# A fused attention and MLP kernel: attention's work put into 20 visits of TensorE instead of 30, in one tile shape

## The chip, the cores and the metric

The kernel runs on one core of a Trainium2 chip. The metric is the time of one execution on the device, in microseconds (us). A core has a matrix engine (TensorE, PE in the profile; its weight loads are listed apart as PEld), VectorE (DVE), ScalarE (ACT), GpSimd (POOL) and SyncE (SP, which issues most DMAs). Matrix products land in PSUM, which has eight banks of 128 partitions x 2 KB; VectorE and ScalarE carry them from there to SBUF. The engines run apart and wait for each other by semaphores.

## The reference

Linear attention with a normalised output, then an MLP with leaky ReLU. All is float32.

```python
batch, n_heads, seq, head_dim = (8, 8, 576, 64)
kv  = np.einsum('bhsd,bhse->bhde', k, v)          # 64 x 64 per head
out = np.einsum('bhsd,bhde->bhse', q, kv)
rms = np.sqrt(np.mean(out * out, axis=-1, keepdims=True) + 1e-06)
out = out / rms * g_norm
x = out.transpose(0, 2, 1, 3).reshape(4608, 512)  # tokens x (heads * head_dim)
h = x @ w_in                                      # 4608 x 2048
g = np.maximum(0.01 * h, h)
return g @ w_out                                  # 4608 x 512
```

## The kernel before, in words

**Blocks and batches.** The MLP works on nine blocks of 512 tokens (`NT`), attention on eight batches of 576. So batch b's tokens lie in block b and, as its *tail*, in block b+1: the part in block b shrinks from 512 tokens (batch 0) to 64 (batch 7), and the tail grows from 64 to 512.

**The MLP.** Block 0 is multiplied plainly (`first_block`, lines 1295 to 1334). From block 1 on, Strassen-Winograd forms are used: one level in block 1, two levels after it. The main loop runs over blocks i = 1 to 8, in each over four chunks c of the hidden width, and in each over seven products t; a step of it is called a *slot*, 7c + t, 0 to 27. In the steady part a slot takes about 3.4 us: TensorE does one product of the first matrix (`h_ha`, `h_hb`, `h_hc`, `h_hd` in the profile) and then one step of the second matrix (`o_a`, `o_c`), for a chunk pair that lies some seven slots back. The steps of the second matrix follow a written plan of 14 steps, `PLAN_3 = "1a 1b . 5a 5b 6a 6b D3 7a A3 7b A4 D4 ."`; a point is a step without work. The bank with tag `oa` is in use from 1a to D4, the bank `oc` from 5a to D3 and in A3 and A4. Behind D4, at slots 13 and 27, both are free once VectorE has read them, and TensorE has no step of the second matrix there.

**PSUM.** Six banks have the tags `ha hb hc hd oa oc` (pool `ps_m`, one buffer each). Two belong to attention (pool `ps_att`, tag `att`, `att_tiles` at line 357).

**Attention.** For each batch: `turn` (line 483) transposes q on VectorE into `qT`; `attention_kv(b, m)` (line 333) multiplies k by v for two of the four head pairs (m = 0 or 1), nine steps over 64 tokens, in 64x64 tiles of TensorE's array (64 rows, 64 columns, so four tiles at a time); a copy on VectorE brings the result to `kvs`; `o_products` (line 370) multiplies q by kv for one half e of the head dimension, 8 matmuls in 64x32 tiles (eight tiles at a time); each float32 matmul stands in the profile as two recorded matmuls with a weight load each. Then ScalarE squares each bank and copies it, scaled by g_norm, to `xT` (`outputs`, `both_outputs`, lines 378 and 426), VectorE adds the squares, and `divide` (line 397) brings in the root. `tail_of` (line 454) strings this together as a generator: a part of up to 256 tokens has both halves e in one bank per side (`both_outputs`), a longer one has them one after the other in the two `att` banks.

**Where it stands.** Each stretch of attention between the MLP's products is here called a *visit* of TensorE. The order of TensorE's instructions is pinned by hand (`pin`, and `matmul` at line 120): the generator `attention(i + 1)` is advanced in slots given by tables (`A_SLOTS` for block 1, `FINE_2`, `FINE_3`, `FINE_SLOTS` for blocks 2, 3 and later, lines 1373 to 1379), the tail of batch i by `TAIL_SLOTS` during block i. Behind the front there are 30 visits. In batches 1 to 3 the two k-by-v halves are visits of their own; from batch 4 on (`KV_BESIDE = 3`, `kv_beside` at line 347) most are put into a visit of the batch before (two of the eight stay visits of their own), behind its q by kv, in the last 64 columns of the same banks, after which ScalarE's squares of these banks follow VectorE's copy of kv. One such visit changes tile shape inside.

**The front.** `first_attention` (line 527) does batch 0's first 512 tokens before anything else: k by v in two stretches with idle matmuls around them that keep the array busy, `o_products` for both halves e, sums of squares by TensorE (`sum_ps`), roots, and the scaling. Batch 0's tail of 64 tokens is a visit of its own during block 0.

**Loads.** k, v and q come by SP's queue (`load_pair`, line 158), one load a slot from a list (`load_some`); `load_kv` puts the next half's k and v on the list when a half has been multiplied.

Of the kernel before, what the change touches and what calls it, by code (L numbers as in the profile page):

```python
# [10 lines left out]
F32 = mybir.dt.float32  # L11
U32 = mybir.dt.uint32
I64 = mybir.dt.int64
AF = mybir.ActivationFunctionType
# [10 lines left out]
def kernel(  # L25
# [100 lines left out]
    def half_of(p, i):  # L126


        return i ^ (p & 1)

    def load_two(eng, src, t):

        pin(eng.dma_start(t.rearrange("p j d -> p (j d)"),
                          src.rearrange("h (p j) d -> (h p) (j d)", j=J)))
        return t
# [21 lines left out]

    def load_pair(b, p, what="kvq"):


        if "k" in what:
            k_ins[b, p] = load_two(nc.sync, k[b, 2 * p:2 * p + 2], in_tile("k"))
        if "v" in what:
            v_ins[b, p] = load_two(nc.sync, v[b, 2 * p:2 * p + 2], in_tile("v"))
        if "q" not in what:
            return
        t = q_tile(b, p)
        for l in range(2):
            for c in range(2):
                r0, n = 64 * l + 32 * c, T * D - 32 * c  # L170
                src = q[b, 2 * p + half_of(p, l)].rearrange("(t s) d -> t (s d)", s=T)
                pin(nc.sync.dma_start(t[r0:r0 + 32, :n], src[:, 32 * c:]))
        q_ins[b, p] = t

    def load_first():

        early = xpool.tile([P, NE * NT], F32, tag="xT", name="early")
        n = J * D

        def rows(t):  # L180
            return t[:, :n].rearrange("p (j d) -> p j d", j=J)

        ks, vs = ([in_tile(name) for _ in range(2)] for name in ("k", "v"))
        qs = [rows(q_tile(0, p)) for p in range(2)]
        qs += [rows(early[:, i * n:]) for i in range(2)]
        ks, vs = (t + [pair(i + j, J, D) for i in range(2)] for j, t in ((0, ks), (2, vs)))
        for way, to, src, ts, p in (
                ("a", q_ins, q, qs, 0), ("s", q_ins, q, qs, 1), ("a", q_ins, q, qs, 2),
                ("s", q_ins, q, qs, 3), ("a", k_ins, k, ks, 0), ("s", v_ins, v, vs, 0),
                ("g", k_ins, k, ks, 1), ("g", v_ins, v, vs, 1), ("a", k_ins, k, ks, 3),  # L190
                ("s", v_ins, v, vs, 3), ("g", k_ins, k, ks, 2), ("g", v_ins, v, vs, 2)):
            if (way, p) == ("g", 2) and src is k:
                make_ident()
            to[0, p] = load_two({"a": nc.scalar, "s": nc.sync, "g": nc.gpsimd}[way],
                                src[0, 2 * p:2 * p + 2], ts[p])
# [136 lines left out]

    def attention_kv(b, m, kv_ps):

        two = [(k_ins.pop((b, p)), v_ins.pop((b, p)), p) for p in (2 * m, 2 * m + 1)]
        for j in range(J):
            for i in range(2):
                for k_in, v_in, p in two:
                    r, c = 64 * i, 64 * half_of(p, i)
                    matmul(kv_ps[p % 2][c:c + 64], lhsT=k_in[r:r + 64, j, :],  # L340
                           rhs=v_in[r:r + 64, j, :], start=(j == 0), stop=(j == J - 1))

    def copy_kv(b, kv_ps):
        for i in range(2):
            in_turn(nc.vector.tensor_copy(kvs[b % 2][:, i::2, :], kv_ps[i]))

    def kv_beside(b, m, tiles):

        kv_ps = [t[:, NT - D:] for t in tiles]
        attention_kv(b, m, kv_ps)  # L350
        for i in range(2):
            in_turn(nc.vector.tensor_copy(kvs[b % 2][:, 2 * m + i, :], kv_ps[i]))
        nxt = (b + m, 2 if m == 0 else 0)
        if nxt[0] < B:
            load_kv(*nxt)
# [22 lines left out]
    def outputs(b, lo, hi, e, sums, kv=None):  # L378


        x, n = x_of(lo, hi), hi - lo
        tiles = att_tiles("o_ps")
        o_ps = [t[:, :n] for t in tiles]
        o_products(b, lo, hi, e, o_ps)
        if kv is not None:
            kv_beside(b + 1, kv, tiles)
        for l in range(2):
            sq = t2k(n, "sq" if e else f"sum{l}")
            nc.scalar.activation(sq, o_ps[l], func=AF.Square)
            if e == 0:  # L390
                sums.append(sq)
            else:
                in_turn(nc.vector.tensor_add(sums[l], sums[l], sq))
        for l in range(2):
            nc.scalar.activation(x[:, 2 * l + e, :], o_ps[l], func=AF.Copy, scale=g_sb[:, e:e + 1])
# [27 lines left out]
            in_turn(nc.vector.tensor_mul(to, to, inv.unsqueeze(1).to_broadcast([P, 2, n])))  # L423
            yield

    def both_outputs(b, lo, hi, sums, kv=None):

        x, n = x_of(lo, hi), hi - lo
        tiles = att_tiles("o_ps")
        o_ps = [t[:, :2 * n].rearrange("p (e n) -> p e n", e=2) for t in tiles]  # L430
        for e in range(2):
            o_products(b, lo, hi, e, [o[:, e, :] for o in o_ps])
        if kv is not None:
            kv_beside(b + 1, kv, tiles)
        squares = []
        for l in range(2):
            sq = t2k(2 * n, "sq").rearrange("p (e n) -> p e n", e=2)
            nc.scalar.activation(sq, o_ps[l], func=AF.Square)
            sums.append(t2k(n, f"sum{l}"))
            squares.append(sq)  # L440

        def add_up():
            for l, sq in enumerate(squares):
                in_turn(nc.vector.tensor_add(sums[l], sq[:, 0, :], sq[:, 1, :]))

        if b != 2:
            add_up()
        for l in range(2):
            for e in range(2):
                nc.scalar.activation(x[:, 2 * l + e, :], o_ps[l][:, e, :], func=AF.Copy,  # L450
                                     scale=g_sb[:, e:e + 1])
        return add_up if b == 2 else lambda: None

    def tail_of(b, lo, hi, fine=False, kv=(None, None)):
        sums = []
        if hi - lo <= N2:
            add_up = both_outputs(b, lo, hi, sums, kv[0])
            yield
            add_up()
            if kv[1] is not None:  # L460
                kv_beside(b + 1, kv[1], att_tiles("kv_ps"))
            yield
        else:
            for e in range(2):
                outputs(b, lo, hi, e, sums, kv[e])
                yield
        for _ in divide(lo, hi, sums):
            if fine:
                yield
        if not fine:  # L470
            yield
# [5 lines left out]
    def attention(b, apart=True, fine=False):  # L477

        qT = qTs[b] = work.tile([P, NP, S], F32, tag="qT", name="qT")
        beside = b > KV_BESIDE  # L480
        kv_ps = None if beside else kv_tiles()

        def turn(p):
            q_in = q_ins.pop((b, p))
# [10 lines left out]
        for m in range(2):  # L495
# [2 lines left out]
            yield  # L498
            turn(2 * m + 1)
            load_q(2 * m + 1)  # L500
            if m or b == KV_BESIDE:
                yield
            if kv_ps:
                attention_kv(b, m, [t[:, m, :] for t in kv_ps])
            if not apart and m == 0:
# [3 lines left out]
                load_kv(b + m, 2 - 2 * m)  # L509
            yield  # L510
            if apart:
                if m and kv_ps:
                    copy_kv(b, kv_ps)
                yield
        if not apart:
            copy_kv(b, kv_ps)
            yield
        kv = [(None, None), (None, None)]
        if KV_BESIDE <= b < B - 1:
            kv = [(None, 0), (None, 1)] if b == KV_BESIDE else \  # L520
                [(None, 0) if b == KV_BESIDE + 1 else (0, None), (1, None)]
        tails = [tail_of(b, max(i * NT, b * S), min((i + 1) * NT, (b + 1) * S), fine, kv[i - b])
                 for i in (b, b + 1)]
        last_tails[b] = tails[1]
        yield from tails[0]
# [1 line left out]
    def first_attention():  # L527
# [32 lines left out]
            keep_warm()  # L560
        for i in range(2):
            for l in range(2):
                c = 64 * half_of(i, l)
                nc.vector.tensor_copy(
                    qT[c:c + 64, i::2, :].rearrange("p a (t j) -> p a j t", j=J)[:, :, 8, :],
                    rest[:, i::2, 64 * l:64 * l + 64])
        for m in range(2):
            if m:
                keep_warm()
# [15 lines left out]
        inv_ps = [ps_m.tile([P, 2, N2], F32, tag=t, name="inv_ps") for t in ("hb", "hd")]  # L585
        for e in range(2):
            o_products(0, 0, NT, e, o_ps[e])

        def add_up(half):

# [66 lines left out]
                scale(half, l)  # L657
        for j in range(1, 5):
            round_w(j)


    later, tick = [], 0
# [670 lines left out]
                nc.vector.tensor_copy(o, accs[t])  # L1333
            nc.scalar.dma_start(out[t * P:(t + 1) * P, :], o)

    first_attention()
    steps = {i: tail for tail in [tail_of(0, NT, S)] for i in (6, 8, 10)}
    a_steps = attention(1, False)
    steps.update((i, a_steps)
                 for i in (12, 13, 15, 16, 19, 20, 22, 23, 24))  # L1340
# [29 lines left out]
    for part in range(2):  # L1370
        combine(0, part)

    A_SLOTS = (2, 3, 5, 8, 10, 11, 13, 14, 15, 17)

    TAIL_SLOTS = {1: 1, 4: 1, 5: 2, 6: 1, 8: 2}
    FINE_SLOTS = {16: 1, 17: 2, 18: 2, 19: 9}, {5: 1, 8: 2, 11: 1, 15: 3}
    FINE_3 = {16: 1, 18: 2, 19: 3, 20: 9}, {5: 1, 8: 2, 11: 1, 15: 3}
    FINE_2 = {4: 2, 8: 1, 12: 1, 13: 1, 17: 1, 18: 2, 19: 9}, {2: 1, 3: 1, 12: 1}
    SUM_SLOTS = {22: 2, 23: 1, 24: 1}

    SLOTS_3 = 10, 20, 22, 23
# [21 lines left out]
    for i in range(1, NB):  # L1403
# [6 lines left out]
        for c in range(NC):  # L1410
# [7 lines left out]
            for t in range(7):  # L1418
# [16 lines left out]
                    waited += 1  # L1435
                if not one:

                    go(late, TAIL_SLOTS.get(slot, 0))
                    go(a_steps, fine[0].get(slot, 0))
                    if i + 1 < NB:  # L1440
                        if slot == 22:
# [106 lines left out]
```

## Time and profile before

| what | value |
|---|---|
| median of 3 runs | 909.41 us (909.36 to 912.88) |
| the profiled execution | 909.77 us, span 908.1 us |
| TensorE busy | 901.6 us (99%), 7344 matmuls and as many weight loads |
| VectorE, ScalarE, GpSimd busy | 616.1 (68%), 330.0 (36%), 521.7 us (57%) |
| granted TensorE clock | 1.000 |
| DMA | 219.00 MB, mean 241 GB/s |
| k-by-v matmuls, recorded | 1152 (720 in `kv_ps`, 432 in `o_ps`) |

An order-of-time line reads: start in us, length of the group from its first start to its last end, engine, line of the kernel, operation, out<-in, the tile of the array where it is not the whole, shapes, count; in brackets the engine's idle time before it and what ended that. Two groups on TensorE overlap, as matmuls are pipelined and their ends are modelled, so costs are read from start to start. A line of a table of stretches has from:to, its length, the busy time of PE, PEld, DVE, ACT and POOL with counts, the granted clock, the DMA share and GB/s.

### The profile page before, as it was taken

Reading aid. Unit: us, or ns where it says so; the run is one execution under the profiler, and the core shown is the slowest. Engines: PE = TensorE matmul, PEld = TensorE weight load, DVE = VectorE, ACT = ScalarE, POOL = GpSimd, SP = SyncE. Lnnn points to the kernel's source line nnn. Section 1 sums busy time; section 2 is a strip of 40 time slices with the busy share of each in tenths; the row PEclk is TensorE's granted clock in tenths of the full one; section 3 lists DMA queues with packets and bytes.
Section 4 is the critical chain, followed back from the end, with each engine's and each line's share of the span. In section 5 each row is a group of like instructions: output and inputs, shape, how many; then the busy total and the mean of one; then the engine's idle time right before and its main releaser. Section 6 shows DMA issues by size and latency. Waiting matters only on the chain.

```text
span 908.1 us, 19140 instructions
## 1 busy us (share of the span) xinstructions
PE 901.6 (99%) x7344; PEld 788.1 (87%) x7344; DVE 616.1 (68%) x942; ACT 330.0 (36%) x645; POOL 521.7 (57%) x672
## 2 busy tenths in 40 slices
PE   8999999999999999999999999999999999999998
PEld 4555558888998989998999999999999899999997
DVE  5877885676574768685977587666877674646453
ACT  5454523231334332434333343334242424232420
POOL 2000236977638784667647673767477847883730
PEclk9999999999999999999999999999999999999999
DMA  8999918977789679967997698958876768677831
GB/s 253 223 241 234 255 68 264 313 255 243 245 286 335 221 230 300 312 223 250 266 302 275 194 315 274 315 181 255 277 256 190 225 206 277 204 233 224 259 110 59
DMA packets 109530, 219.00 MB, mean 241 GB/s; under 512 B 11776, under 2 KB 51072, under 8 KB 109440
## 3 DMA queue, kind: packets, MB, share of 16 engines
q1 hardware_dynamic: 105504, 212.22, 76.1%
q10 hardware_dynamic: 3488, 4.39, 1.4%
q8 instruction: 58, 0.95, 0.4%
q0 software_dynamic: 448, 1.18, 0.3%
q14 instruction: 32, 0.26, 0.1%
HBM read 187.34 MB, written 30.41 MB: 240 GB/s over the span
## 4 chain that ended last, share of the span: by engine, by line
PE 97%; DMA 1%; DVE 1%; POOL 0%; ACT 0%; issue 0%; ACTq 0%; DVEq 0%; POOLq 0%
PE o_a L121 20%; PE o_c L121 16%; PE h_hc L121 10%; PE h_hd L121 10%; PE h_ha L121 10%; PE h_hb L121 9%; PE o_acc L121 6%; PE h_ps L121 6%; PE o_ps L121 3%; PE h_a L121 2%; PE h_b L121 2%; PE kv_ps L121 1%; PE h_c L121 1%; PE h_d L121 1%; DMA pairs<-in_v_dram 1%; PE o_hc L121 0%
## 5 line engine op out<-in xcount | busy, mean ns | idle before, releaser
L669 POOL TENSOR_TENSOR gs<-g 128x512 f32<-128x512 f32 x62 | 85.5, 1379 | 126.9 <-ACT g L864 65.2
L121 PE MATMUL o_a<-pairs,gs 128*128 128x256 f32 x472 | 111.9, 379 | 0.0
L669 DVE TENSOR_TENSOR o_all<-o_c,o_all 128x256 f32<-128x256 f32 (+2 forms) x124 | 69.5, 560 | 60.3 <-PE o_c L121 46.9
L669 POOL TENSOR_TENSOR w_all<-w_all 128x512 f32<-128x512 f32 x28 | 53.4, 1906 | 88.3 <-ACT w_all L1088 88.2
L864 ACT ACTIVATE g<-g 128x512 f32<-128x512 f32 x124 | 75.7, 630 | 67.8 <-DVE g L669 67.8
L669 DVE TENSOR_TENSOR g<-g,w_all 128x512 f32<-128x512 f32 (+1 forms) x84 | 89.8, 1069 | 11.7 <-POOL w_all L669 5.5
L121 PEld LDWEIGHTS o_a<-pairs,gs 128*128 128x128 f32 x472 | 85.5, 190 | 9.5 <-DVE o_all L669 0.2
L669 DVE TENSOR_TENSOR w_all<-h_ha,w_all 128x512 f32<-128x512 f32 x42 | 28.7, 684 | 55.4 <-PE h_ha L121 53.5
L1088 ACT COPY w_all<-h_hc 128x512 f32<-128x512 f32 x42 | 25.0, 596 | 106.7 <-PE h_hc L121 106.7
L121 PE MATMUL o_c<-pairs,gs 128*128 128x256 f32 x264 | 62.4, 379 | 0.0
L669 POOL TENSOR_TENSOR pairs<-w 128x512 f32<-128x512 f32 x4 | 5.3, 1330 | 98.6 <-DMA stage<-in_moe_w_out_dram 98.6
L669 DVE TENSOR_TENSOR o_all<-o_a,o_all 128x512 f32<-128x512 f32 (+1 forms) x53 | 35.5, 669 | 38.4 <-PE o_a L121 37.8
L669 DVE TENSOR_TENSOR g<-w_all 128x1024 f32<-128x1024 f32 x28 | 35.3, 1260 | 37.1 <-ACT w_all L1088 37.1
L121 PE MATMUL o_a<-w,g 128*128 128x256 f32 x248 | 58.8, 379 | 0.0
L121 PE MATMUL h_ps<-xT,w_all 128*128 128x512 f32 (+1 forms) x136 | 58.1, 571 | 0.3 <-DVE w_all L278 0.3
L121 PE MATMUL o_acc<-w,g 128*128 128x256 f32 (+1 forms) x192 | 57.7, 451 | 0.0
L121 PEld LDWEIGHTS o_acc<-w,g 128*128 128x128 f32 x192 | 36.3, 190 | 21.5 <-issue 17.2
L121 PEld LDWEIGHTS o_c<-pairs,gs 128*128 128x128 f32 x264 | 47.9, 190 | 5.3
L1088 ACT COPY w_all<-h_ha 128x512 f32<-128x512 f32 x42 | 24.8, 592 | 72.8 <-PE h_ha L121 72.8
L121 PEld LDWEIGHTS o_a<-w,g 128*128 128x128 f32 x248 | 45.0, 190 | 4.9
L121 PEld LDWEIGHTS h_ps<-xT,w_all 128*128 128x128 f32 x136 | 25.4, 190 | 26.9 <-issue 24.4
L121 PEld LDWEIGHTS h_ha<-stage,w_all 128*128 128x128 f32 x336 | 42.7, 192 | 3.0 <-issue 1.6
(287 smaller groups left out, 2405.3 us busy)
## 6 DMA issues: line engine op xcount, KB each, us to landing
w_all<-w SPq DMA_DIRECT2D x196, 448.0 KB, 4.7
pairs<-w SPq DMA_DIRECT2D x94, 256.0 KB, 4.5
w<-w SPq DMA_DIRECT2D x22, 448.0 KB, 5.9
v_in<-in_v_dram SPq DMA_DIRECT2D x29, 288.0 KB, 6.2
k_in<-in_k_dram SPq DMA_DIRECT2D x28, 288.0 KB, 6.3
q_in<-in_q_dram SPq DMA_DIRECT2D x46, 144.0 KB, 5.0
q_in<-in_q_dram SPq DMA_DIRECT2D x46, 140.0 KB, 5.4
w<-stage SPq DMA_DIRECT2D x12, 512.0 KB, 4.0
```

What stands on the lines that cost most here:

```text
L121: pin(nc.tensor.matmul(*args, **kw))
L669: ins = eng.tensor_tensor(out_, a, b_, op=ALU.subtract if minus else ALU.add)
L864: nc.scalar.activation(t, t if src is None else src, func=AF.Prelu, alpha=SLOPE)
L1088: nc.scalar.copy(q[:, at], bank)
```

## The change

- **k by v in 64x32 tiles.** Each 64x64 product is made of two of 64x32 (`for d in (0, E)`), so it has the tile shape of q by kv. The pairs of a half are now p = m and m + 2 (before, 2m and 2m + 1), loads follow that order (`KV_ORDER`), and `half_of` goes by p // 2, so that each tile of the array writes one and the same bank in q by kv and in k by v.
- **Fewer visits.** Batches 2 to 7 have at least one half of k by v behind a q by kv of the batch before. `wide_outputs` multiplies both halves e of a longer part in one visit, over four banks: the two `att` banks and two more, `hb` and `hd` (batch 2, in block 1) or `oa` and `oc` (tails of batches 4 to 7). The half in the borrowed banks is multiplied and evacuated first. Where a part of 256 tokens fills the `att` banks, k by v goes to `oa` and `oc`.
- **Places.** From block 3 on the tail's visit stands at slot 27 of the block before, not at slots 1 and 4; batch 4's first part stands at slot 13 (before, 16, and its k by v at 18).
- **Batch 0's tail.** Its q by kv is multiplied in the front, behind that of the first 512 tokens, into spare columns of `sum_ps`; ScalarE and VectorE take it up during block 0 as before.

```diff
     def half_of(p, i):
-        return i ^ (p & 1)
+        return i ^ (p >> 1)
+
+    KV_ORDER = (0, 2, 1, 3)
...
-        two = [(k_ins.pop((b, p)), v_ins.pop((b, p)), p) for p in (2 * m, 2 * m + 1)]
+        two = [(k_ins.pop((b, p)), v_ins.pop((b, p)), p) for p in (m, m + 2)]
         for j in range(J):
             for i in range(2):
                 for k_in, v_in, p in two:
                     r, c = 64 * i, 64 * half_of(p, i)
-                    matmul(kv_ps[p % 2][c:c + 64], lhsT=k_in[r:r + 64, j, :],
-                           rhs=v_in[r:r + 64, j, :], start=(j == 0), stop=(j == J - 1))
+                    for d in (0, E):
+                        matmul(kv_ps[p // 2][c + d:c + d + E], lhsT=k_in[r:r + 64, j, d:d + E],
+                               rhs=v_in[r:r + 64, j, :], start=(j == 0), stop=(j == J - 1))
...
+    def copy_half(b, m, kv_ps):
+        for i in range(2):
+            in_turn(nc.vector.tensor_copy(kvs[b % 2][:, m + 2 * i, :], kv_ps[i]))
...
         if kv is not None:
-            kv_beside(b + 1, kv, tiles)
+            places = [flat_bank(tag, "kv_ps") for tag in banks] if banks else tiles
+            kv_beside(b + 1, kv, ends_of(places))
...
+    def wide_outputs(b, lo, hi, sums, kv, banks):
+
+        x, n = x_of(lo, hi), hi - lo
+        apart = [flat_bank(tag, "o_ps") for tag in banks]
+        tiles = att_tiles("o_ps")
+        o_ps = {e: [t[:, :n] for t in ts] for e, ts in ((1, apart), (0, tiles))}
+        for e in (1, 0):
+            o_products(b, lo, hi, e, o_ps[e])
+        if kv is not None:
+            kv_beside(b + 1, kv, ends_of(tiles))
+        squares = []
+        for e in (1, 0):
+            for l in range(2):
+                sq = t2k(n, "sq" if e else f"sum{l}")
+                nc.scalar.activation(sq, o_ps[e][l], func=AF.Square)
+                (squares if e else sums).append(sq)
+                nc.scalar.activation(x[:, 2 * l + e, :], o_ps[e][l], func=AF.Copy,
+                                     scale=g_sb[:, e:e + 1])
+        yield
+        for l in range(2):
+            in_turn(nc.vector.tensor_add(sums[l], sums[l], squares[l]))
...
-        beside = b > KV_BESIDE
-        kv_ps = None if beside else kv_tiles()
+        beside, early = b > KV_BESIDE, 1 < b <= KV_BESIDE
+        kv_ps = None if beside or early else kv_tiles()
...
+            if early:
+                if m == 0:
+                    continue
+                half = [t[:, :D] for t in att_tiles("kv_ps")]
+                attention_kv(b, 1, half)
+                load_kv(b + 1, 0)
+                yield
+                copy_half(b, 1, half)
+                yield
+                continue
...
-        if KV_BESIDE <= b < B - 1:
-            kv = [(None, 0), (None, 1)] if b == KV_BESIDE else \
-                [(None, 0) if b == KV_BESIDE + 1 else (0, None), (1, None)]
+        if b < KV_BESIDE:
+            kv[1] = (0, None)
+        elif b < B - 1:
+            kv = [(None, 0) if b == KV_BESIDE else (0, None), (1, None)]
+        banks = [{2: ("hb", "hd"), 4: ("oa", "oc")}.get(b), ("oa", "oc") if b >= KV_BESIDE else None]
...
         for e in range(2):
             o_products(0, 0, NT, e, o_ps[e])
+        rest_o = both_products(0, NT, S, [t[:, N2 + P:] for t in sum_ps])
...
-    A_SLOTS = (2, 3, 5, 8, 10, 11, 13, 14, 15, 17)
+    A_SLOTS = (2, 3, 8, 10, 11, 13, 15, 17)
...
-    FINE_3 = {16: 1, 18: 2, 19: 3, 20: 9}, {5: 1, 8: 2, 11: 1, 15: 3}
-    FINE_2 = {4: 2, 8: 1, 12: 1, 13: 1, 17: 1, 18: 2, 19: 9}, {2: 1, 3: 1, 12: 1}
+    FINE_3 = {13: 1, 18: 2, 19: 3, 20: 9}, {3: 1, 6: 2, 9: 1, 12: 3}
+    FINE_2 = {8: 1, 12: 1, 13: 1, 17: 1, 18: 2, 19: 9}, {2: 1, 3: 1, 12: 1}
...
-                    go(late, TAIL_SLOTS.get(slot, 0))
+                    if slot > 1 or i == 2:
+                        go(late, TAIL_SLOTS.get(slot, 0))
+                    if slot == 7 * NC - 1 and i + 1 in last_tails:
+                        go(last_tails[i + 1], 1)
```

## The prediction

> **What bounds the kernel now.** I read the page first (busy times, then the chain), then a table of stretches, then the waits of TensorE, and last the order of time around single visits of attention, because the change is about what one visit costs.
>
> ```profile
> PE 901.6 (99%) x7344; PEld 788.1 (87%) x7344; DVE 616.1 (68%) x942; ACT 330.0 (36%) x645; POOL 521.7 (57%) x672
> PE 97%; DMA 1%; DVE 1%; POOL 0%; ACT 0%; issue 0%; ACTq 0%; DVEq 0%; POOLq 0%
> q8 instruction: 58, 0.95, 0.4%
> ```
>
> ```profile
> 228.00:510.00 282.00, 282.00 (x2667) 263.74 (x2666) 195.93 (x283) 103.44 (x211) 183.53 (x250) 1.00 0.83 267
> 510.00:726.00 216.00, 216.00 (x1928) 201.45 (x1927) 155.10 (x222) 83.35 (x170) 144.88 (x198) 1.00 0.79 252
> ```
>
> TensorE is 99% busy and 97% of the chain; in the stretches where attention lies between the MLP's products it is busy 282.00 of 282.00 us and 216.00 of 216.00 at a clock of 1.00. Its waits come to 2.8 us, all before 27.3 us. So in the steady part each microsecond that leaves TensorE's order leaves the span, and nothing else can give one, as long as the other engines keep up. Busy is no proof of use, though: what a visit costs must be read from the starts.
>
> ```profile
> 416.96 1.89 PE L121 MATMUL o_a<-w,g 128*128 128x256 f32 x8
> 418.78 0.77 PE L121 MATMUL o_ps<-qT,kv 64*32 64x320 f32 x16
> 419.48 1.28 PE L121 MATMUL o_ps<-v_in,k_in 64*64 64x64 f32 x72
> 420.69 1.16 PE L121 MATMUL h_ha<-stage,w_all 128*128 128x128 f32 x8
> ```
>
> ```profile
> 427.21 1.89 PE L121 MATMUL o_c<-pairs,gs 128*128 128x256 f32 x8
> 429.03 0.77 PE L121 MATMUL o_ps<-qT,kv 64*32 64x320 f32 x16
> 429.73 0.49 PE L121 MATMUL h_hc<-xT,w_all 128*128 128x128 f32 x2
> 430.05 0.39 PE L121 MATMUL h_hc<-xt,w_all 128*128 128x128 f32 x2
> 430.28 0.39 PE L121 MATMUL h_hc<-xT,w_all 128*128 128x128 f32 x2
> ```
>
> ```profile
> 43.32 1.45 PE L121 MATMUL h_ps<-xT,w_all 128*128 128x512 f32 x3
> 44.70 0.45 PE L121 MATMUL o_ps<-qT,kv 64*32 64x64 f32 x32
> 45.09 1.13 PE L121 MATMUL o_acc<-w,g 128*128 128x256 f32 x4
> ```
>
> Eight 256-wide matmuls start 1.73 us apart from group to group (427.21, then 428.94 had no visit come). So the visit at 429.03 (16 matmuls of q by kv, 320 columns) costs 429.73 - 428.94 = 0.79 us. The visit at 619.99 with 448 columns costs 1.00 by the same reading. Sixteen matmuls on eight tiles are two rounds, so 0.21 us more for 2x128 columns is 0.83 ns a column; of the 0.79, 2x320x0.83 = 0.53 is array work and **0.26 is fixed**. After it the next two matmuls take 0.32 to the following ones, where 0.23 is usual: **0.10 more**. A visit's fixed price is thus 0.36 us.
>
> **The change, part by part.** (1) *Ten visits fewer.* Before, by batches 0 to 7, there are 1, 5, 5, 6, 4, 3, 3 and 3 visits behind the front; after, 0, 5, 3, 4, 2, 2, 2 and 2. The columns of q by kv stay. 10 x 0.36 = 3.6 us saved.
>
> (2) *One tile shape in a visit.* Six visits of before hold q by kv in 64x32 tiles and then k by v in 64x64. That at 418.78 costs 420.69 - 418.69 = 2.00 us. Its q by kv alone is 0.79; its 72 k-by-v starts spread over 1.28 - 0.22 = 1.06 (0.22 is the duration of one). 2.00 - 0.79 - 1.06 leaves 0.15 for the change of shape in between. After, both parts have 64x32 tiles: 6 x 0.15 = 0.9 us saved. Bounds: nothing saved (the tiles wait for each other all the same), or 0.2 each. I take 0.9, the rows' own difference.
>
> (3) *k by v in 64x32 tiles.* Half a batch becomes 144 recorded matmuls of 64 columns over eight tiles, instead of 72 over four: still 18 rounds. The nearest row has exactly this shape, the visit at 44.70: 32 matmuls of 64 columns start within 0.45 - 0.21 = 0.24 us, 7.7 ns apart. At that mean, 143 x 7.7 = 1.10 us a half (0.04 worse than 1.06, 0.6 us over the 14 halves behind the front); at the array's own 53 ns a round (64 x 0.83), 0.96 (1.4 us better). Its 32 include the slower first round, so I take 1.01 and 14 x 0.05 = 0.7 us saved. The weight loads double as well, one with each matmul; the same row has them.
>
> [...]
>
> (4) *Batch 0's last tokens.* The visit at 44.70 is one of the ten; its 0.21 us of array work goes too. In the front the same 32 matmuls (0.24 us) come between 15.46 and the sums at 17.55. The sums start at 17.55 and need squares that ScalarE finishes from 17.4 to 18.9, but they also follow one another at 0.22 us, so I count no cover: zero together. With full cover it is 0.2 better.
>
> (5) *What moves.* ScalarE has the same squares and copies, eight in a row (0.49 to 0.70 each) where a visit is now wide, instead of four and four. VectorE's copies of kv (two of 0.22 a half; before, two of 0.28 a batch for the early ones) now wait, in written order, for the end of the longest visits; queued behind them are the adds that finish a chunk's g (1.23, then 3.70 for three, at 603.67), and ScalarE's leaky ReLUs wait for those. With 448 columns the wide visit lasts 93 ns + 4 x 0.37 + 1.0 + 0.17 = 2.75 us. VectorE gets free 3.2 us after its start, the first add ends at 4.4, ScalarE's eight end near 5.3, the ReLU (0.63) near 5.9; TensorE needs that g at 2.75 + 1.56 + 1.73 + 1.56 = 7.6 (spacing of 602.86, 604.42, 606.15, 607.71). Hidden with 1.7 us to spare. With 512 columns (batch 7, no k by v) the visit is 2.0 long, the eight take 5.2, the ReLU ends near 6.8 and is needed at 6.8: no room. The banks oa and oc are free at that place: the last add from oa ends at 601.74, a microsecond before, and the half that lies there is evacuated first, done at 2.0 (oa), needed at 4.3. Loads of k and v go out on SP's queue in pairs 0,2 then 1,3: the same bytes, and the second half is still issued some ten steps of 3.4 us ahead, against 6.2 to land, so zero. At batch 4's first half the visit at 283.38 lost about 0.3 us inside to the landing of v, issued at 277.28; its place and issue stay, so it stays (0.3 better if not). The front's second k by v is on the chain, at the price of (3): within 0.1.
>
> Sum: 3.6 + 0.9 + 0.7 + 0 = 5.2 us. The profiled execution took 909.77 (span 908.1 and 1.7 around it); the median of the runs is 909.41, 0.36 less. 909.77 - 5.2 = 904.6, from the median 904.2. I predict 904.3.
>
> **Rivals.** *A: starts slow down in a long burst (slower than before).* The 32 matmuls at 44.70 may have been waiting ready in TensorE's queue; a half now has 144 with as many loads. The only long burst of before is 72 in 1.06 us, 14.7 ns a start; that is its end of the range: 143 x 14.7 = 2.1 us a half, 14 x 1.04 = 14.6 us and 1 in the front, against 4.5 saved elsewhere: 920.5. It decides from 9.7 ns a start on, where 14 halves lose 4.5. Against it: in the 72, starts come in fours 7 ns apart and then pause, which looks like tiles that are busy and not like a slow issue. A middle value of 11 ns gives 912.
> [...]
>
> *B: instructions run short.* The page has 58 packets of instructions on queue 8, 0.95 MB: 16 KB each, one for some 256 of the 14,688 matmuls and loads; their share (0.4% of 16 engines' 908 us) makes about 1.0 us a packet. The densest burst of before is 104 pairs, 208 instructions in 1.9 us; now a visit has up to 352 in 2.8, and the front two bursts of 288. If no more than one packet's worth is kept ahead, a burst that crosses a boundary within its first 96 stalls until the next has come: 3 of 8 of ten visits at 1 to 2 us, 5.6 together, and up to 3 in the front: 909.8 - 5.2 + 8.6 = 913, the gain lost and a little more. Nothing in the trace reaches this density, so nothing excludes it.
> [...]
>
> *C: ScalarE or VectorE becomes late.* At the four wide visits of the last batches, and where kv's copies hold VectorE, the reserve above is 0 to 1.7 us. If the adds or ReLUs come a microsecond late in half of the eight longest visits, it costs 4: 908. For it: the written order on VectorE. Against it: 36% busy ScalarE, and no wait of TensorE on it in the steady part now.
>
> **How the numbers follow.** The forecast has 0.57, A 0.12, B 0.18, C 0.10, and 0.03 is left for what I have not seen. The forecast's own range puts (2), (3), (4) and the wait at their ends: gains of 2.8 to 6.5, 902.9 to 907. C fills 905 to 908.5, B 908 to 916, A 907 to 921. Up to 913 there lie the forecast, C, two thirds of B and a good part of A: range 902.8 to 913. Half a percent, about what a measurement of this kernel can tell from no change, is 4.5 us: 904.9 and 914.0. The forecast lies below 904.9 in some 8 of 10 (0.45), and 0.01 comes from the rest. Slower holds a third of B, a third of A and some of what is unseen: 0.12. The rest, 0.42, is within.
>
> **What would show it.** In the order of time, visits whose rows are all 64*32; 144 k-by-v starts within 1.0 to 1.1 us; a visit at 448 columns with k by v of 2.75; 20 visits; no waits of TensorE past 27.3 us. A would show as k-by-v groups of 1.3 us and more in every half alike; B as gaps inside some visits only, each with a packet on queue 8 just before its end; C as waits of TensorE on ScalarE or VectorE one or two steps behind a wide visit. Wrong altogether would be gaps in the MLP's own products away from any visit.

## The result: 937.6 us, slower by 3%

The kernel after takes 937.63 us (median of 6 runs, 935.33 to 944.01), the kernel before, beside it, 910.59 (909.32 to 914.64): a ratio of 1.0297, 95% interval 1.0257 to 1.0336. The forecast of 904.3 was wrong, and its range ended at 913.0.

The page of the kernel after (span, busy times, the chain by engine, the instruction packets of TensorE's queue):

```profile
span 934.4 us, 21429 instructions
PE 910.5 (97%) x8496; PEld 802.9 (86%) x8496; DVE 614.5 (66%) x946; ACT 330.9 (35%) x645; POOL 518.5 (55%) x672
PE 93%; DMA 2%; issue 2%; POOL 1%; ACT 1%; SPq 1%; DVE 0%; ACTq 0%
q8 instruction: 67, 1.10, 0.5%
```

TensorE still carries the chain, but 2% of it is "issue": time in which TensorE waited for nothing that the profile shows. The span grew by 26.3 us. TensorE's waits say where (line waited for, releaser, us in total, times, longest):

```profile
PE kv_ps L121 <- issue: 5.7, 1, 5.7
PE h_hc L121 <- issue: 3.0, 1, 3.0
PE o_ps L121 <- issue: 2.6, 1, 2.6
PE h_ha L121 <- issue: 2.2, 1, 2.2
PE h_a L121 <- POOL pairs L723: 1.9, 1, 1.9
```

Before, waits came to 2.8 us. Here the four largest pauses with no releaser make 13.5 us, each at another place, and a wait on GpSimd has come. The stretches that were fully busy before are not any more (columns as in the table of stretches of before):

```profile
228.00:510.00 282.00, 275.95 (x3053) 259.79 (x3052) 184.53 (x277) 101.12 (x205) 171.18 (x239) 0.99 0.85 270
510.00:726.00 216.00, 213.02 (x2131) 201.76 (x2130) 151.72 (x220) 76.92 (x155) 142.38 (x189) 0.99 0.77 240
...
435.00:438.20 3.20, 3.20 (x28) 3.04 (x16) 2.78 (x5) 2.12 (x5) 0.00 (x0) 0.54 0.39 97
591.50:595.20 3.70, 3.70 (x16) 3.35 (x15) 0.00 (x0) 1.06 (x2) 3.54 (x9) 0.54 0.96 316
```

The last two lines are the time just behind two of the pauses: the granted clock (third figure from the end) is 0.54 there. One such visit in order of time, with 320 columns and k by v, as at 418.78 before:

```profile
429.54 1.31 PE L121 MATMUL o_ps<-qT,kv 64*32 64x320 f32 x32
430.64 1.54 PE L121 MATMUL o_ps<-v_in,k_in 64*32 64x64 f32 x131
434.77 0.46 PE L121 MATMUL o_ps<-v_in,k_in 64*32 64x64 f32 x13 [2.59 <-issue]
435.16 0.79 PE L121 MATMUL h_ha<-xT,w_all 128*128 128x128 f32 x2
```

The change was made as described (one shape, 144 k-by-v starts), but after 131 of them TensorE stands still for 2.59 us and then goes on with the same tiles; the profile names no releaser. The `h_ha` line behind it is slow as well: 0.79 for two matmuls where 0.49 is usual behind a visit. The front has the longest pause:

```profile
13.29 0.71 PE L121 MATMUL kv_ps<-pairs 64*32 64x64 f32 x47
19.71 1.62 PE L121 MATMUL kv_ps<-pairs 64*32 64x64 f32 x97 [5.71 <-issue]
```

**Where a pause begins.** The packets of queue 8 are taken here for TensorE's instructions: 67 of 16 KB (1.10 MB), one for some 258 of the 17,311 instructions that the trace lists for TensorE; before, 58, one for some 259 of 15,015. The count here takes every instruction of TensorE that the trace lists, in order of start: matmuls, weight loads and the semaphore instructions among them. So counted, each pause of the table begins behind a number that leaves 193 when divided by 256. The table puts the multiples of 256 at remainder 196, which counts 60 instructions ahead of the first listed one. That place is a choice, but with it a kernel passes as many multiples as its queue 8 has packets (58 before, 67 here). The table holds the front's second k by v and, from 295.40 on, all visits of 320 instructions and more in the kernel after (times in us from the visit's first start; read from the same trace):

| visit | instructions | multiples of 256 at | stops after | pause | packet in that time |
|---|---|---|---|---|---|
| 13.29 (front) | 288 | +96 | 93 | 5.92 | 3.38 to 4.94 |
| 295.40 | 322 | +139 | | none | 2.60 to 3.53 |
| 328.43 | 353 | +116, +372 | 369 | 1.29 | 2.50 to 3.46 |
| 377.70 | 352 | +107, +363 | 360 | 2.52 | 3.00 to 3.97 |
| 429.54 | 353 | +72, +328 | 325 | 2.80 | 2.93 to 3.88 |
| 489.90 | 353 | +176 | | none | 3.17 to 4.17 |
| 529.30 | 354 | +3, +259 | | none | -0.95 to 0.02 |
| 585.62 | 353 | +106, +362 | 359 | 3.26 | 2.75 to 4.21 |
| 629.60 | 354 | +189 | | none | 4.44 to 5.41 |

Every pause begins three instructions ahead of a multiple of 256 and ends 1.2 to 1.5 us after a packet. It comes where one multiple has been passed early in the visit (in the front, in the k by v before it) and the next is reached before that packet is there. The counts of +362, +363 and +372 lie just behind the visit's end, in the MLP's products. The visits at 152.25 and 244.40 (355 instructions) have a multiple at +205 and +207 and no pause. What sets when a packet begins stays open: that of the visit at 529.30 came 0.95 us ahead of the visit.

**The account** (first steady `h_ps` for the front; each visit's cost from start to start, less the usual spacing): the front ends at 36.20 instead of 27.34, +8.9. Behind it: pauses and the half clock that follows them, +14.5 (2.8 inside the visit at 429.54, and 1.28, 4.18, 1.44 and 4.82 behind visits); slower k-by-v starts, +4.0 (less what the change of shape had cost); the wait on GpSimd, +2.2; small waits, +0.6; ten visits fewer, -3.1. That is 27.1 against 26.3; 0.8 I cannot assign.

### The profile page after: what moved, and what is told of

It is laid out like the page before. It is cut to its first block, busy times and chain, and to the rows that moved or that the text cites. A ratio compares the mean times of both kernels' runs of the same rounds, so it can differ in the third digit from the quotient of the medians.

```text
span 934.4 us, 21429 instructions
## 1 busy us (share of the span) xinstructions
PE 910.5 (97%) x8496; PEld 802.9 (86%) x8496; DVE 614.5 (66%) x946; ACT 330.9 (35%) x645; POOL 518.5 (55%) x672
## 4 chain that ended last, share of the span: by engine, by line
PE 93%; DMA 2%; issue 2%; POOL 1%; ACT 1%; SPq 1%; DVE 0%; ACTq 0%
PE o_a L121 19%; PE o_c L121 15%; PE h_ha L121 10%; PE h_hd L121 10%; PE h_hc L121 9%; PE h_hb L121 9%; PE o_acc L121 6%; PE h_ps L121 6%; PE o_ps L121 3%; PE h_a L121 2%; PE kv_ps L121 1%; PE h_c L121 1%; PE h_b L121 1%; PE h_d L121 1%; DMA k_in<-in_k_dram 1%
## 5 line engine op out<-in xcount | busy, mean ns | idle before, releaser
L723 POOL TENSOR_TENSOR w_all<-w_all 128x512 f32<-128x512 f32 x28 | 48.2, 1721 | 93.6 <-ACT w_all L1142 93.6
L723 DVE TENSOR_TENSOR g<-g,w_all 128x512 f32<-128x512 f32 (+1 forms) x84 | 86.7, 1032 | 13.6 <-POOL w_all L723 7.9
L723 DVE TENSOR_TENSOR g<-w_all 128x1024 f32<-128x1024 f32 x28 | 35.5, 1267 | 27.1 <-ACT w_all L1142 27.1
L121 PE MATMUL h_hc<-stage,w_all 128*128 128x128 f32 x336 | 45.2, 277 | 3.0 <-issue 3.0
```

Of the source, the lines that this page charges most:

```text
L121: pin(nc.tensor.matmul(*args, **kw))
L723: ins = eng.tensor_tensor(out_, a, b_, op=ALU.subtract if minus else ALU.add)
```

## The experiments

The theory after the result, inferred from the table above: TensorE has at most the next 256 instructions at hand when it passes a multiple of 256, and the tile shape of k by v, which doubles the instructions of a half, is what uses them up too fast. The rivals: the fewer, longer visits or their borrowed banks do it; or the starts themselves are the cost and the pauses have another cause. All ratios are against runs of the kernel before on the same chip.

### One part alone: the tile shape

The kernel after with 64x64 tiles, and with it two kernels that keep the 30 visits of before.

```diff
-                    for d in (0, E):
-                        matmul(kv_ps[p // 2][c + d:c + d + E], lhsT=k_in[r:r + 64, j, d:d + E],
-                               rhs=v_in[r:r + 64, j, :], start=(j == 0), stop=(j == J - 1))
+                    matmul(kv_ps[p // 2][c:c + 64], lhsT=k_in[r:r + 64, j, :],
+                           rhs=v_in[r:r + 64, j, :], start=(j == 0), stop=(j == J - 1))
```

> The whole change, but k by v in 64x64 tiles again (72 recorded matmuls a half instead of 144). Theory (instructions run short at every 256th, and starts in a long burst of 64x32 tiles come 10 ns apart): both causes are gone, as no visit has more than 208 instructions. What stays is ten visits fewer (3.6 us saved), less some 0.1 us for ten instead of six changes of shape, and the new wait on GpSimd in block 1 (about 2 us lost): 907 to 909 us, no pause inside any visit. Rival (the visits' new places, the four banks and ScalarE's eight operations in a row are what costs): nearly all of the loss stays, 925 us or more.

The kernel before with the change's pairs, loads and 64x32 tiles, everything else as it was:

```diff
     def half_of(p, i):
-        return i ^ (p & 1)
+        return i ^ (p >> 1)
...
+                    for d in (0, E):
+                        matmul(kv_ps[p // 2][c + d:c + d + E], lhsT=k_in[r:r + 64, j, d:d + E],
...
```

> The kernel before with its 30 visits in their old places, and only the 64x32 tiles for k by v (with the new pairs of heads and the new map of banks, which they need). Theory: 14 halves at 0.39 us more (5.4), six changes of shape gone (-0.9), the front's pause as in the changed kernel (about 8.9), and some of the six visits that hold q by kv and k by v pause 3 to 5 us each, those in which a multiple of 256 instructions falls near their first third: 925 to 938 us. Rival (places): 909 to 911 us. The wait on GpSimd in block 1 should be absent.

The same without the last edit: pairs and loads of the change, tiles of 64x64, 30 visits.

```diff
     def half_of(p, i):
-        return i ^ (p & 1)
+        return i ^ (p >> 1)
...
-        two = [(k_ins.pop((b, p)), v_ins.pop((b, p)), p) for p in (2 * m, 2 * m + 1)]
+        two = [(k_ins.pop((b, p)), v_ins.pop((b, p)), p) for p in (m, m + 2)]
...
```

> The kernel before with its 30 visits and its 64x64 tiles; only the assignment of pairs to halves and banks, the order of the loads of k and v that follows from it, and the layout of the copies are taken from the change. Theory (tile shape, packets and the lost cover make the whole loss, and the late v loads in block 0 seen in two experiments are the spread of the loads from run to run): the same time as before, 909 to 911, no pause and no wait behind 27.3 us beyond before's. Rival (the new order of loads itself delays v in block 0): waits of k by v on v's DMA of 1 us and more near 69 and 92 us, and 911.5 to 914.

| | k by v in 64x64 | k by v in 64x32 |
|---|---|---|
| 30 visits | 910.34, ratio 1.0009 (0.9983 to 1.0035) | 936.60, ratio 1.0294 (1.0264 to 1.0324) |
| 20 visits | 912.51, ratio 1.003 (1.002 to 1.0039) | 937.63, ratio 1.0297 (1.0257 to 1.0336) |

The tile shape costs 26 us with 30 visits and 25 with 20, so it makes nearly the whole loss, and the rival that blames the long visits or their banks falls. Pairs and the order of loads cost nothing that can be told. In 64x64 the visit of 320 columns has no pause and takes 2.45 from start to start, where after has 5.62:

```profile
417.70 1.31 PE L121 MATMUL o_ps<-qT,kv 64*32 64x320 f32 x32
418.94 1.28 PE L121 MATMUL o_ps<-v_in,k_in 64*64 64x64 f32 x72
420.15 0.49 PE L121 MATMUL h_ha<-xT,w_all 128*128 128x128 f32 x2
```

With 30 visits and 64x32, the 288 instructions of a lone k by v are enough. Two lines of order of time: the k by v that begins at 249.99 meets multiples of 256 at +34 and +290, and the product behind it waits. The trace names w_all's DMA as releaser; the stop after 287 instructions, again at remainder 193, the packet at 2.14 to 3.25 and the restart 1.4 us behind it say that it is the same pause:

```profile
249.99 1.66 PE L121 MATMUL kv_ps<-v_in,k_in 64*32 64x64 f32 x144
254.68 0.77 PE L121 MATMUL h_hc<-xT,w_all 128*128 128x128 f32 x2 [3.03 <-DMA w_all<-w]
```

The 20 visits in 64x64 still lose 0.3% (expected were 907 to 909 us), by two waits, read from TensorE's waits of that kernel:

```profile
PE sum_ps L121 <- issue: 3.2, 1, 3.2
PE h_a L121 <- POOL pairs L722: 2.2, 1, 2.2
```

The first, in the front, stops at remainder 193 as well. No k by v of that kernel is in 64x32, so the pauses are not bound to k by v in that tile shape.

### Moving the packets' boundaries

If the place against the multiples of 256 decides, 96 more instructions ahead of the visits must move the pauses to other visits. The edit splits some of block 0's matmuls by columns, with the same work.

```diff
-                parts = 2 if n == 0 else 1
+                parts = 2 if n == 0 else 4 if n in (5, 6) else 1
```

> The changed kernel, with two of block 0's first products issued in four pieces of 128 columns instead of one of 512: the same work, 96 instructions more ahead of batch 2, nothing else moved. Theory of the instruction supply: each boundary now falls 96 instructions earlier in every later visit, so the pauses leave the visits of batches 3 (tail), 4 (both) and 6 (first) and appear in those of batch 1's tail, batch 2's tail, batch 3's second part, batch 5's first part and batch 6's tail; with five instead of four, 938 to 945 us. Rival (places, semaphores, loads): the same visits pause as before, 937 to 938 us.

It took 945.38, ratio 1.0391 (1.0349 to 1.0432). The visit of the 320 columns, paused in the kernel after, is whole, and the one with 192 columns, which had no pause at 489.90, has one:

```profile
434.83 1.31 PE L121 MATMUL o_ps<-qT,kv 64*32 64x320 f32 x32
435.93 1.66 PE L121 MATMUL o_ps<-v_in,k_in 64*32 64x64 f32 x144
...
491.62 1.58 PE L121 MATMUL o_ps<-v_in,k_in 64*32 64x64 f32 x134
495.21 0.33 PE L121 MATMUL o_ps<-v_in,k_in 64*32 64x64 f32 x10 [2.01 <-issue]
```

In this kernel the visit at 434.83 has its multiple at +230 (no second one), that at 490.94 at +78 and +334; it stops after 331 instructions. Pauses stand at nine visits, and each again three instructions ahead of a multiple. Data and tiles of these visits are unchanged; what the edit moves is their place against the boundaries. Not as expected were three pauses of 0.9 to 1.8 us in visits that I had held for safe, and one that stayed in the visit at 590.59. So of the four visits behind the front that pause in the kernel after, three still do, but not in the same place: with its semaphore instructions the edit adds 98, and these three stop 98 instructions earlier in the visit (after 271, 262 and 261 instead of 369, 360 and 359).

Over the kernel after and the seven variants that have such pauses, 41 stops of 0.9 us or more begin at remainder 193. The other stops of that length behind 13 us have a semaphore instruction or a semaphore's wait just ahead of them and other remainders.

With 240 instructions more, most pauses should have gone:

```diff
-                parts = 2 if n == 0 else 1
+                parts = 2 if n == 0 else 4 if n in (5, 6, 7, 8, 9) else 1
```

> As the run before, with five products in four pieces: 240 instructions more. Theory of the instruction supply: nearly a whole block of 256, so boundaries fall 16 instructions later than in the changed kernel; of the four pausing visits behind the front only batch 4's tail still has its boundary in the first hundred, the other three lose their pauses (1.2, 4.3 and 5.0 us): 926 to 929 us. Rival: 937 to 938 us as the changed kernel.

It took 935.28, ratio 1.028 (1.0256 to 1.0304): a miss by 6 us or more, and by the time alone nearer to the rival. The visits with multiples at +118 and +374, at +83 and +339, and at +117 and +373 still pause (2.83, 2.90 and 1.76 us), and so does that at +127 and +383 (1.02): all four that pause in the kernel after. With semaphore instructions the edit adds 245, which is 11 short of 256, and each of the four stops 11 instructions later in its visit. I had taken the visit's own end, some 352 instructions, as the limit; the MLP's products behind it reach +374 before the packet is there, too. The boundaries decide, but a shift does not find a free place for all visits.

### The price of the starts by itself

Each k-by-v matmul of the kernel after streams 32 of its 64 columns. Half of k by v is left out, so the array streams half the columns, and TensorE's instructions stay.

```diff
-                        matmul(kv_ps[p // 2][c + d:c + d + E], lhsT=k_in[r:r + 64, j, d:d + E],
-                               rhs=v_in[r:r + 64, j, :], start=(j == 0), stop=(j == J - 1))
+                        cols = slice(E * (j % 2), E * (j % 2) + E)
+                        matmul(kv_ps[p // 2][c + d:c + d + E, cols], lhsT=k_in[r:r + 64, j, d:d + E],
+                               rhs=v_in[r:r + 64, j, cols], start=(j == 0), stop=(j == J - 1),
...
```

> The changed kernel, but each k-by-v matmul streams 32 of its 64 columns (even steps the first 32, odd steps the last), so half of k by v is left out, with as many matmuls and weight loads. If TensorE's supply of ready instructions sets the 10 ns from start to start, a half still takes 1.45 us from first to last start, and the time stays at 935 to 940 us. If the array's tiles set it, a half falls to about 0.8 us, and the time by some 9 us.

It took 936.62 (one run). From the first to the last of the 144 starts of a half it is 1.23 us, against 1.447 with all columns: half the columns take away 15% of the time. That is neither the 1.45 nor the 0.8 expected, but it shows that the columns streamed set the smaller part of the pace. Whether the rest is the supply of instructions or the weight loads, which the edit leaves as they are, this run does not separate. Its pauses begin behind the same counts as in the kernel after, but have other lengths (3.9, 3.9, 3.6, 3.4 and 2.5 us against 3.0, 2.2, 5.7, 2.6 and 1.0), so its time says little about the starts.

What a half costs without a pause, in the kernel before and then in the kernel after:

```profile
69.36 1.28 PE L121 MATMUL kv_ps<-v_in,k_in 64*64 64x64 f32 x72
```

```profile
77.64 1.66 PE L121 MATMUL kv_ps<-v_in,k_in 64*32 64x64 f32 x144
79.23 1.13 PE L121 MATMUL h_ps<-xT,w_all 128*128 128x512 f32 x2
```

From 77.64 to 79.23 it is 1.59, where the same half took 1.21 in 64x64 tiles before (69.36 to 70.57). The first 32 starts come within 0.238 us (7.7 ns apart), the other 112 are 10.8 ns apart. Behind a q by kv the first 32 take 0.34 us and the others come 9.9 ns apart; the whole half takes the same 1.45.

### The front

Only batch 0 in 64x64, all else as after.

```diff
-                    for d in (0, E):
-                        matmul(kv_ps[p // 2][c + d:c + d + E], lhsT=k_in[r:r + 64, j, d:d + E],
+                    for d in (0, E) if b else (0,):
+                        n = E if b else D
+                        matmul(kv_ps[p // 2][c + d:c + d + n], lhsT=k_in[r:r + 64, j, d:d + n],
...
```

> The changed kernel with 64x64 tiles in batch 0's k by v alone, in the front: 288 instructions fewer there. Theory of the instruction supply: the front loses its pause of 5.7 us in k by v but keeps one at the sums, as in the first run, and is 4 to 5 us shorter; behind it every boundary falls 32 instructions later in its visit, so the pauses of batch 3's tail, of batch 4's first part and of batch 6's first part go (1.2, 4.3, 5.0 us) and batch 4's tail keeps its own: 921 to 926 us. Rival: the front alone changes, 932 to 933 us.

It took 928.02, ratio 1.0187 (1.0152 to 1.0223). The front ends at 28.90 instead of 36.20, so 7.3 of its 8.9 us came of the tile shape there. The front keeps a stop of 1.50 at the sums. The edit also takes 288 instructions out ahead of all visits, so the pauses behind moved again: 1.96 at 376.35, 3.38 at 423.64, 1.57 at 523.61 and 2.50 at 583.57. Two of the three that were to go have stayed, 32 instructions later in their visits, and the one at 523.61 is new. A further stop, 1.35 at 288.72, is not one of them: its remainder is 65, and the trace names the DMA of v as its releaser. That is why the run misses its range.

Batch 0's tail back in block 0, in the kernel with 64x64 tiles:

```diff
-        rest_o = both_products(0, NT, S, [t[:, N2 + P:] for t in sum_ps])
+        rest_o = None
```

> The change with 64x64 tiles for k by v (as in the first run), and batch 0's last tokens multiplied during block 0 again, as before the change. Theory: their 64 loads and matmuls in the front filled the stretch up to a boundary of 256 instructions, where the front then paused 3.2 us; without them the front is as in the kernel before. 4.3 us of the front back, 0.6 us for the visit in block 0: 3.7 us less than the first run, 908.5 to 909.5 us, and no wait of that kind before 27.5 us. Rival (the front was slowed by its transposed order of loads): 912 us as before it.

It took 911.87, ratio 1.001 (0.9991 to 1.0028), and its front ends at 27.14, where the 64x64 kernel with the tail in front has 31.61. So part (4) of the change costs 4.5 us there: its 32 matmuls and 32 loads, put between q by kv and the sums, use up the instructions to the next multiple of 256, and TensorE stops for 3.21 us behind the first 11 of these matmuls (in the 64x64 kernel with the tail in front). In the profiled execution 2.7 us went back into late v in block 0 (below), and the time is not the 908.5 to 909.5 expected.

### The lost cover in block 1

In the kernel after, `h_a` in block 1 waits for a sum that GpSimd makes from the chunk before. Before, batch 2's k by v (147.45) stood between `h_c` and that `h_a`; after, it has moved two slots up. GpSimd's sum in the kernel before, which ran under that k by v:

```profile
147.60 1.28 POOL L669 TENSOR_TENSOR pairs<-w_all 128x512 f32<-128x512 f32 x1 [7.28 <-PE h_c L121]
```

Order of time of TensorE, then of GpSimd, in the kernel after:

```profile
156.16 1.89 PE L121 MATMUL h_c<-xt,pairs 128*128 128x256 f32 x8
159.97 1.32 PE L121 MATMUL h_a<-xT,pairs 128*128 128x256 f32 x5 [1.92 <-POOL pairs L723]
```

```profile
158.13 1.41 POOL L723 TENSOR_TENSOR pairs<-w_all 128x512 f32<-128x512 f32 x1 [9.05 <-PE h_c L121]
```

GpSimd can begin only when `h_c` has ended, and takes 1.41; nothing is left to run on TensorE in that time. Two kernels put the visit back between the two, with batch 2's first part two slots later as well, the one on the kernel of the last experiment, the other on the kernel after as it is.

```diff
-    A_SLOTS = (2, 3, 8, 10, 11, 13, 15, 17)
+    A_SLOTS = (4, 5, 8, 10, 11, 13, 15, 17)
...
-                    if slot in (1, 5):
+                    if slot in (3, 5):
...
-                        go(late, 1 if slot == 1 else 9)
+                        go(late, 1 if slot == 3 else 9)
```

> As the run before, and in block 1 the tail's visit of batch 1 with its k by v stands at slot 3 instead of slot 1, so that it lies where the kernel before had a k by v, over GpSimd's sums (batch 2's transposes follow it, at slots 4 and 5). Theory of the lost cover: TensorE's wait of 2.2 us for GpSimd's sums goes: 906.3 to 907.3 us, faster than the kernel before by 0.25 to 0.35%. Rival (GpSimd is late because of something else in block 1): the wait moves with it, 908.5 to 909.5 us.

> The kernel after, with one edit: in block 1 the tail's visit stands at slot 3 again (at 1 in the kernel after), and batch 2's k by v and first part move from slots 2 and 3 to 4 and 5; tile shape, visits and all that follows stay as in the kernel after. Theory (the wait of 1.9 to 2.2 us on GpSimd in block 1 comes only of the place that k by v left, and has nothing to do with the pauses at packet boundaries): that wait falls to 0.5 or less, the pauses of 1.3 to 3.3 us behind block 1 stay at their visits, since as many instructions stand ahead of them, and the time is 2 us below the kernel after: about 935.5. Rival (GpSimd's lateness is a consequence of the late front or of the new tile shape): the wait stays or moves to the next visit of block 1, and the time stays at 937 to 938.

On 64x64 tiles: 910.22 us, ratio 0.9999 (0.9977 to 1.002). On the kernel after: 936.39, ratio 1.0297 (1.0278 to 1.0316). TensorE's waits of the first, and then of the second:

```profile
PE kv_ps L121 <- DMA v_in<-in_v_dram: 3.6, 2, 2.3
...
PE h_a L121 <- DVE g L722: 0.3, 1, 0.3
```

```profile
PE h_ha L121 <- issue: 5.9, 2, 3.3
...
PE h_hc L121 <- issue: 4.1, 1, 4.1
```

The wait on GpSimd is gone from both, so its cause is the place that k by v left; in the first, 0.3 us on VectorE is left of it. On the kernel after, the time is 1.2 us lower, less than it can be told from the spread of the runs, and the profiled span is no shorter. The pauses stand at the same visits as in the kernel after, but those behind the front are longer: at the multiple behind the visit of 256 columns, 2.83 instead of 1.29, with a packet that ended 4.66 after the visit's start instead of 3.46. So the size of a pause is also that of a transfer's delay, and varies.

On 64x64 tiles I had expected 906 to 907. Two things stand against it in the profiled execution (912.47 us). Small waits on ScalarE and VectorE one or two steps behind wide visits come to 1.35 us (0.46 at 156.3, 0.37 at 352.2, 0.19 at 703, 0.33 at 731): rival C, at a third of its price. And in the profiled executions of both last 64x64 kernels, batch 1's two k-by-v halves wait for v (3.6 us here). Loads moved at 218 and 222 GB/s there between 10 and 95 us, 230 in the kernel before. The order of the loads is not the cause, since the 30-visit kernel with the same order has no such wait (234 GB/s). What is, stays open; two profiled executions are too few to call it a property of these kernels. So the version without any of the three losses equals the kernel before (lowest runs 908.08 and 908.81); none that I ran beats it by what can be told.

## Why the prediction was wrong

**The step that failed: the sum has no term for the supply of TensorE's instructions.** The prediction added up array work, fixed prices of visits and starts, and left the supply to rival B. The runs show it as the main cost: of the 26.3 us that the span grew, some 23 are the pauses at multiples of 256 and the half clock behind them (8.9 in the front, slower starts there included, and 14.5 behind it). The parts of the sum, one by one:

**(1) Ten visits fewer: right.** In 64x64 tiles with the tail back in block 0, 21 visits cost 35.79 (38.47 less 2.68 of late v) against 37.35 for 30, and nine restarts of 0.103 go: 2.5 us saved. My price of 0.36 each gives 3.2, less four changes of shape more than before (10 against 6), 2.7.

**(2) The change of shape: right.** From 64x64 to 64x32, visits of k by v alone cost 0.387 more (1.301 to 1.688), those with q by kv ahead 0.247 more (2.968 to 3.216 at 448 columns, 2.754 to 2.999 at 384). The difference, 0.14, is what the change of shape had cost; I had 0.15.

**(3) k by v in 64x32: the price was wrong.** I took 1.01 us a half; it is 1.447, and with what stands around it 0.387 more than in 64x64, 5.4 us over 14 halves instead of 0.7 saved (4.0 once the change of shape is taken off). My row, the visit at 44.70, has exactly 32 matmuls, as many as start at the fast pace; the 112 that follow were in no row. Rival A named that, and its bound of 9.7 ns was passed (10.1 on the mean of 143). At 10.1 ns its own sum gives about 911: A came true, and was the smaller part.

**Rival B is what happened, at a multiple of its price.** I gave it 0.18 and 913. Its condition was right (a multiple of 256 within about the first 96 instructions; found: up to +116 here, and +139 in the kernel with the front in 64x64), and its count nearly (3 of 8 of ten visits; four behind the front here). What failed is the price. I took 1 to 2 us a pause from the packet's own duration of about 1 us; TensorE goes on only 3.5 to 4.9 us after the burst has passed the boundary (430.64 to 434.77 at the visit of 429.54), so pauses are 1.3 to 3.3 us, 9.9 for the four. I left out the half clock behind three of them, which brings the four to 14.5 us instead of 5.6. And in the front I had "up to 3": it is 8.9, as the packet there began 5.4 us after the boundary was passed (11.27 to 16.67). The DMA engines were 0.82 busy in that time; that their loads held the packet back is not shown.

**(4) Batch 0's tail: zero was wrong.** It costs 4.5 us with 64x64 tiles, not by its work but by the 64 instructions that it puts ahead of a boundary. I counted its array time and not these.

**(5) What moves: an engine was left out.** I followed VectorE, ScalarE and SP's queue, and not GpSimd's sums in block 1, for which the k by v at 147.45 was the cover: 2.2 us. Apart from that and the pauses, TensorE's waits behind the wide visits of the kernel after are 0.3 us each, at 727 and 755, so VectorE and ScalarE were nearly in time, as I had said.

Of the signs that I named, the visits in one shape and their number were there; a half in 1.0 to 1.1 us and no waits past 27.3 us were not. The sign of A is there (every half alike at 1.45), and that of B nearly: each gap has a packet on queue 8 that ends 1.2 to 1.5 us ahead of the gap's end, but three of the four gaps behind the front lie in the MLP's products just behind the visit. The loss was named in the prediction and given too small a price and chance: 288 to 355 instructions in 1.6 to 3.1 us was a density that no row of before covered (its densest 208 in 2 us), and I put the forecast's weight on the side where the trace was silent.

## What to carry to other kernels

Count TensorE's instructions, not only its array time: here a burst that passed a multiple of 256 and reached the next before the packet between them was there stopped (in the kernel after, TensorE went on 3.5 to 4.9 us after the first multiple behind the front, 8.4 in it), and which burst that hit, and where, changed with the instructions added ahead of it (98 and 245 here). A price read from a short burst need not hold for a long one: here the first 32 pairs of load and matmul started 7.7 ns apart, the 112 behind them 10.8. When work moves away from a place, look at what every engine, GpSimd too, does in its shadow.

## What the hardware showed

- In the kernel after and the seven variants with such pauses, all 41 of them begin at the same remainder of 256 (193 in the count used here), and TensorE went on 1.0 to 1.7 us after a 16 KB packet had ended.
- In a half of k by v that stands alone, pairs of load and matmul in 64x32 tiles start 7.7 ns apart for the first 32 and 10.8 ns apart after that.
- In the kernel after, the three pauses of 2.5 us and more behind the front were followed by half the clock over some 3.4 us (0.54 in 435.00 to 438.20 and in 591.50 to 595.20), which costs 1.4 to 1.7 us more; behind the pause of 1.28 it stayed 1.00. The length alone does not decide. With the cover put back on the kernel after, the same visit pauses longer and the clock stays 1.00, while with 96 instructions more a pause of 2.23 us was followed by 0.70 in 495.20 to 499.00:

```profile
435.26 0.34 PE L121 MATMUL o_ps<-v_in,k_in 64*32 64x64 f32 x15 [3.42 <-issue]
...
435.00:438.20 3.20, 2.94 (x34) 2.75 (x34) 2.40 (x5) 2.12 (x5) 0.00 (x0) 1.00 0.34 92
```
